# Spreading the first projections of q and k over the score tiles, and turning the last attention sums on TensorE

## The chip, the cores and the metric

The kernel runs on one core of one Trainium2 chip. The metric is the device time of one execution in microseconds. The engines are called as in the profile: PE (TensorE matmuls), PEld (TensorE weight loads), DVE (VectorE), ACT (ScalarE), POOL (GpSimd) and SP (the sync engine, which issues every DMA of this kernel).

## The reference

Two independent attention blocks, A and B, over 2048 tokens of 640 features, with 32 heads of 20 features; their outputs stand side by side.

```
# A: causal attention in a sliding window of 256 tokens
q, k, v = split(x @ wqkv)                      # (heads, S, 20) each
p = softmax(where(0 <= i - j < 256, q k^T * 20**-0.5, -1e9))
a = concat_heads(p @ v) @ wo
# B: linear attention, not causal
phi = lambda t: where(t > 0, t + 1, exp(t)) + 1e-6
kv, z = phi(k)^T @ v, sum(phi(k))
b = concat_heads(phi(q) @ kv / (phi(q) @ z + 1e-6)) @ wo
out = concatenate([a, b], axis=-1)             # (1, 2048, 1280)
```

Inputs, weights and outputs are bf16.

## The kernel before

The tokens are cut into four blocks of 512, numbered 0 to 3 (the first to the fourth block). Everything that can be is a "chain": five matmuls (one for each 128 of the 640 features) that sum into one of four PSUM buffers called `dense`, and then a copy out by VectorE or ScalarE (`evac`, L258 and L260, which share this work by a running allowance). The four buffers go round in turn, so a chain starts only when the chain four places before it has been copied out; the sums of A's attention (`values`) take their place in this ring too.

A's work: `a_rows` makes the rows of q or k of a block in five chains of 512 columns (`qpad`, `kpad`). A head group of four heads needs its rows at 32 row steps, so the first five of eight groups are ready as they come, and the last three are put together by writing spare rows to DRAM and reading them back (`moves`: four writes at L381, four reads at L390). `a_v` makes the values. `scores` makes one of 76 score tiles: matmuls into the one PSUM tile `S_ps` (L747), the exponential by ScalarE (`p`, L765), and the mask by GpSimd's selects (`p` and `plow`, L778). `values` (L805) sums the tiles of a head group over the keys; VectorE turns the result in 32 by 32 squares (`T`, L816), takes the reciprocal (`recA`), and multiplies (`N` and `Nr`, L832). For a block's first 128 features (`N`) four DMA transposes turn the sums to `oT` (`turn_all`, L844); the last 32 of each quadrant (`Nr`) are turned by VectorE (L851). `a_out` multiplies with wo.

B's work: `b_keys` makes phi of the keys, with ScalarE's exponential (`e`, L285) and two steps on VectorE (L290 and L293); `b_sums` sums keys and tokens, `b_kv` and `b_merge` fold the result into the weights (`wB`); `b_q` makes phi of the queries, turned to tokens by DMA (`tok`, L684); `b_den` makes the denominators (`rden`); `quotients` multiplies them in on VectorE (L719), turns each part back by DMA (`xA`, L723); `b_out` makes the output rows.

The order is written out by hand. Ahead of the loop the kernel loads, regroups the weights of q and k into 32 row steps (`regroup`, L356 to L362), and makes all ten chains of the first block of q and k (`run(a_rows(n, 0))`), and drops its eight reads (`drop`). Then the loop over the 76 tiles issues a tile's scores, the sums of the group that was completed two tiles before, and then "fill": chains and other steps taken from a list `plan`, sorted by a due time in tiles (`at`, `do`, `reads_of`, `divide`), until a credit of columns is used up:

```
rate = (FILL - TAIL + n_values * VALUES) / len(units)
```

So FILL is the number of columns in the plan, and TAIL what is kept for the end. After the last tile `take(7000)` runs more fill while the last exponential and masks are made; then come the last sums, the rest of the fill, and `a_out_last`, the output rows of A's fourth block, in chains of 320 columns. Steps that must not run at once (the second half of phi, a reciprocal, a DMA that waits for a copy) are held for one to three chains (`later`, `soon`, `settle`, `flush`).

Of the kernel before, what the change touches and what calls it, by code (L numbers as in the profile page):

```python
# [20 lines left out]
SB = 512  # L21
TPS = SB // P

FILL = 377960
TAIL = 24000

VALUES = 2200
SPARE = 1200
# [62 lines left out]
def kernel(  # L91
# [135 lines left out]
    def flush(before=None):  # L227

        while later and (before is None or later[0][0] <= before):
            later.pop(0)[1]()  # L230
# [33 lines left out]
    def bank(wide=False):  # L264
        flush(begun[0] - 2)
        begun[0] += 1
        settle(False)
        if wide:
            return dps.tile([P, 2 * SB], BF16, name="dense")
        return dps.tile([P, SB], F32, name="dense")  # L270
# [33 lines left out]
    def banks(g, n):  # L304

        for _ in range(n):
            for c in g:
                yield c
                if isinstance(c, End):
                    break  # L310
# [64 lines left out]
    def moves(n, s, pad):  # L375
# [17 lines left out]
            )  # L393

        reads[n, s] = [(read, j) for j in range(4)]

    def drop(key):
        while reads[key]:
            fn, j = reads[key].pop(0)
            fn(j)  # L400

    def a_rows(n, s):
        i = 0 if n == "q" else 1
        pads, pl, name = (q_pad, qp, "qpad") if n == "q" else (k_pad, kp, "kpad")
        pad = pads[s] = pl.tile([P, NG, SB], BF16, name=name)
        for c in range(KT):
            ps = bank()
            yield from chain(
                ps[:],
                lambda kt: wqk[:, i, kt, c * P : (c + 1) * P],  # L410
                lambda kt: xA[s][:, kt, :],
                SB,
            )
            evac(pad[:, c, :], ps[:])
            if c == KT - 1:
                moves(n, s, pad)
            yield End(SB)
# [74 lines left out]
    def wo_proj(wt, base, oT, s, col0):  # L492
        osb = op.tile([P, TPS, D], BF16, name="osb")

        def done(tb, ps):
            if tb is None:
                evac(osb[:, :, SB:D], ps)
            else:
                evac(osb[:, tb, 0:SB], ps[:])

        yield from tok_rows(oT, wt, base, done)
        dst = out2[s * SB : (s + 1) * SB, col0 : col0 + D]
        soon(
            lambda: nc.sync.dma_start(out=dst.rearrange("(t p) n -> p t n", p=P), in_=osb[:]), 2
        )
# [283 lines left out]
    def values(s, g, held):  # L789


        O_ps = dps.tile([P, SB], F32, name="dense")
        todo = []
        for (_, rel, q0, n, col, step), (p, low) in held:
            if rel == "M":
                own = key(s, q0 // P)
                todo.append((own, low, q0, n, col - LOW, step))
                if own >= 2:
                    todo.append((own - 2, p, q0 + HALF, n, col, step))
            else:  # L800
                todo.append((key(s, rel), p, q0, n, col, step))
        for i, (kb, p, q0, n, col, step) in enumerate(todo):
            at = (kb % TPS * H + 4 * g) * HV
            for j in range(4):
                nc.tensor.matmul(  # L805
                    O_ps[32 * j : 32 * (j + 1), q0 : q0 + n],
                    lhsT=v_flat[kb // TPS % 3][:, at + j * HV : at + j * HV + 32],
                    rhs=columns(p, j, col, n, step),
                    start=(i == 0),
                    stop=(i == len(todo) - 1),  # L810
                    tile_position=(0, 32 * j),
                    skip_group_check=True,
                )

        T = tp.tile([P, SB // 32, 32], F32, name="T")
        nc.vector.transpose(out=T.rearrange("p b e -> p (b e)"), in_=O_ps[:])  # L816
        if s not in norm_A:
            norm_A[s] = (
                np_.tile([P, SB // 32, P], BF16, name="N"),
                np_.tile([P, SB // 32, 32], BF16, name="Nr"),  # L820
            )
        N, Nr = norm_A[s]

        def rest():
            r = sp.tile([P, SB // 32, 1], F32, name="recA")
            nc.vector.reciprocal(out=r[:], in_=T[:, :, DH:HV])
            lo = g * DH
            for dst, a, b in ((N, lo, min(lo + DH, P)), (Nr, max(lo, P), lo + DH)):
                if a >= b:
                    continue  # L830
                at = a - P if dst is Nr else a
                nc.vector.tensor_tensor(  # L832
                    out=dst[:, :, at : at + b - a],
                    in0=T[:, :, a - lo : b - lo],
                    in1=r[:].to_broadcast([P, SB // 32, b - a]),
                    op=ALU.mult,
                )
            if lo < P <= lo + DH:
                oT_A[s] = op1.tile([P, KT, SB], BF16, name="oT")

                def turn_all():
                    for j in range(4):
                        quadrant = slice(32 * j, 32 * (j + 1))
                        nc.sync.dma_start_transpose(  # L844
                            out=oT_A[s][:, j, :].rearrange("p (b e) -> p b e", e=32),
                            in_=N[quadrant].rearrange("p b x -> p (b x)"),
                        )

                soon(turn_all, 2)
            if g == NG - 1:  # L850
                nc.vector.transpose(  # L851
                    out=oT_A[s][:, KT - 1, :], in_=Nr.rearrange("p b e -> p (b e)")
                )

        later.append((begun[0], rest))

    def a_out(s):
        settle()
        yield from wo_proj(wo_sb["A"], 0, oT_A[s], s, 0)

    def a_out_last(s):
        settle()
# [16 lines left out]
    def run(gen):  # L879
        for _ in gen:  # L880
            pass
# [39 lines left out]
    def late_load(n, w):  # L921
# [18 lines left out]
        else:  # L940
# [2 lines left out]
            nc.sync.dma_start(out=wo_sb[n][0:g, 0:KT, :], in_=whole)  # L943
            nc.sync.dma_start(out=wo_sb[n][0 : D - KT * g, KT, :], in_=w[KT * g : D, :])

    for n in "qk":
        run(a_rows(n, 0))
    for n in "qk":
        drop((n, 0))


    plan = []
# [1 line left out]
    def at(t0, t1, gen, n):  # L954
        for i in range(n):
            plan.append((t0 + (i + 0.5) / n * (t1 - t0), gen, i == n - 1))
# [9 lines left out]
    def reads_of(t0, t1, n, s):  # L966
        def one():
            fn, j = reads[n, s].pop(0)
            fn(j)

        do(t0, t1, [one] * 4)
# [1 line left out]
    def divide(t0, t1, s):  # L973
        do(t0, t1, [lambda fn=fn, tb=tb: fn(tb) for fn, tb in quotients(s)])

    for s, tq, tk, tv in ((1, (0, 6), (5, 11), (9, 14.5)), (2, (19, 26), (25, 32), (15, 22)),
                          (3, (36, 41.5), (41, 46), (43, 49))):
        at(*tq, a_rows("q", s), KT)
        reads_of(tq[1] + 1.5, tq[1] + 3.5, "q", s)
        at(*tk, a_rows("k", s), KT)  # L980
        reads_of(tk[1] + 1.5, tk[1] + 3.5, "k", s)
        at(*tv, a_v(s), 2 * TPS)
    for s, t0, t1 in ((0, 2, 9), (1, 8.5, 14), (2, 21.8, 27), (3, 27, 32.5)):
        at(t0, t1, b_keys(s), KT)
    for half, t0, t1 in ((0, 15, 21.5), (1, 33.6, 39.2)):
        at(t0, t1, b_sums(half), KT + 2)
    for s, t in ((0, 4), (1, 9), (2, 23), (3, 24)):
        do(t, t, [lambda s=s: load_tok(s)])
    at(40.4, 42, b_kv(), 2)
    do(42.8, 44.8, [lambda c=c: kv_ready(c) for c in range(3)])  # L990
    for s, tq, td, tx in ((0, (39.5, 45), 47, (49, 51)), (1, (45, 50), 53.4, (55.5, 58)),
                          (2, (51.5, 56.5), 59.6, (62, 64.5)), (3, (58.7, 62.8), 65, (66.5, 68.5))):
        at(*tq, b_q(s), KT)
        at(td, td + 0.1, b_den(s), 1)
        divide(*tx, s)
    at(46.5, 54, b_merge(), 2 * KT)
    for n, s, t0, t1 in (("A", 0, 44.5, 48.5), ("A", 1, 51.5, 55.5), ("B", 0, 55.5, 59.5),
                         ("B", 1, 60.5, 64.5), ("B", 2, 65, 68.8), ("A", 2, 68.8, 72.5),
                         ("B", 3, 72.5, 76)):
        at(t0, t1, (a_out if n == "A" else b_out)(s), KT)  # L1000
    for n, s, t0, t1 in (("B", 1, 3, 8), ("A", 2, 6, 12), ("B", 2, 14, 18), ("A", 3, 16, 24),
                         ("B", 3, 17, 22)):
        parts(t0, t1, n, s)
    for s, t0, t1 in ((0, 2, 33.5), (1, 10, 38.5), (2, 20, 45.5), (3, 26, 51.2)):
        do(t0, t0, [lambda s=s: keep_x(s)])
        do(t1, t1, [lambda s=s: again_x(s)])
    for t, n, w in ((13, "B", 2), (20, "B", 0), (40.6, "A", A_wo), (42, "B", B_wo)):
# [13 lines left out]
    def take(cols):  # L1021
        done = 0.0
        while done < cols:
            try:
                done += next(fill)
            except StopIteration:
                break
        return done
# [26 lines left out]
        credit -= take(credit)  # L1055
    spare[0] = None
    while ready:
        take(7000)
        _, at = ready.popleft()
        values(*at, held.pop(at))  # L1060
        flush()
    for _ in fill:
        pass
    flush()
# [30 lines left out]
```

## Time and profile before

| | |
|---|---|
| three runs | 271.9, 274.4 and 275.42 us, median 274.4 |
| the profiled execution | 271.8 us, of which the span from first to last instruction is 270.1 |
| granted TensorE clock, mean | 0.994 |
| busy: PE, PEld | 254.1 and 142.2 us |
| busy: DVE, ACT, POOL | 164.1, 212.2 and 172.8 us |
| first score matmul | 23.62 us |
| first matmul of the last tile's scores | 248.28 us |
| first chain of A's last output rows | 261.1 us |

Times of the profile count from the first instruction. A busy engine may still be one that works below its best, since ends of matmuls are modelled. A releaser in brackets behind a row is what ended the idle time just before that row. The loop runs from 23.62 us to about 250, 3.0 us for a tile; the front holds the loads and the first chains, and the tail the last output rows.

### The profile page before, as it was taken

To read this page: it belongs to the slowest core of one execution; us is meant where nothing else is said; L and a number is where in the kernel's file an instruction comes from. 1 tells how busy PE (TensorE), PEld (TensorE's weight loads), DVE (VectorE), ACT (ScalarE), POOL (GpSimd) and SP (SyncE) were. 2 spreads that over 40 slices of the span, in tenths; PEclk is the share of its full clock that TensorE was granted. 3 is DMA by queue.
4 is the path that set the end of the run, shared out by engine and by line. 5 is a ranking of instruction groups with operands and counts; after the bars stand their busy time and mean duration, and the time that the engine had idled before them with its cause. 6 is when DMAs were issued, how large, how long until landed. Compare 5 with 4: busy or idle time off the path is not lost.

```text
span 270.1 us, 10767 instructions
## 1 busy us (share of the span) xinstructions
PE 254.1 (94%) x4753; PEld 142.2 (53%) x4753; DVE 164.1 (61%) x268; ACT 212.2 (79%) x290; POOL 172.8 (64%) x211
## 2 busy tenths in 40 slices
PE   8899999899999999999999999999599989967995
PEld 7544445465548455454576455565245564534663
DVE  1532476946312458887544663548948979998742
ACT  2455999998999899987778999999468989876221
POOL 6211768878695867676685889595934977776100
PEclk9999999999999999999999999999979999999999
DMA  7994986797369936021652694307573495467574
GB/s 205 302 264 72 198 209 153 195 203 88 61 101 258 237 140 162 12 47 32 96 173 56 125 123 136 60 22 168 105 173 63 132 137 107 83 120 167 141 156 177
DMA packets 67683, 36.87 MB, mean 137 GB/s; under 512 B 50357, under 2 KB 66613, under 8 KB 67637
## 3 DMA queue, kind: packets, MB, share of 16 engines
q1 hardware_dynamic: 67637, 36.19, 60.6%
q8 instruction: 37, 0.61, 1.0%
q14 instruction: 9, 0.07, 0.1%
HBM read 14.42 MB, written 9.83 MB: 90 GB/s over the span
## 4 chain that ended last, share of the span: by engine, by line
PE 72%; DVE 14%; DMA 4%; POOL 3%; ACT 3%; issue 3%; SPq 1%; DVEq 0%; ACTq 0%
PE dense L275 46%; PE dense L547 9%; PE S_ps L747 9%; PE dense L805 7%; DVE tok L719 3%; DVE e L290 3%; DVE phi L293 3%; DMA wA<-in_A_wqkv_dram 2%; ACT p L765 2%; POOL p L778 2%; DMA xA<-tok 2%; DVE N L832 1%; POOL plow L778 1%; DVE T L816 1%; PE dense L626 1%
## 5 line engine op out<-in xcount | busy, mean ns | idle before, releaser
L778 POOL TENSOR_SCALAR_AFFINE_SELECT p<-p 128x512 bf16<-128x512 bf16 (+1 forms) x152 | 123.1, 819 | 69.6 <-ACT p L765 64.4
L765 ACT ACTIVATE p<-S_ps 128x2048 bf16<-128x2048 f32 x76 | 142.2, 1872 | 22.2 <-PE S_ps L747 21.7
L275 PE MATMUL dense<-xA,wqk 128*128 128x512 bf16 x200 | 49.5, 380 | 0.0
L290 DVE TENSOR_SCALAR e<-e 128x512 bf16<-128x512 bf16 x40 | 28.2, 704 | 29.5 <-ACT e L285 26.2
L778 POOL TENSOR_SCALAR_AFFINE_SELECT plow<-p 128x1024 bf16<-128x1024 bf16 x32 | 39.9, 1248 | 2.2
L275 PEld LDWEIGHTS <-xA 128*128 128x128 bf16 x320 | 26.8, 98 | 23.3 <-DMA xA<-tok 4.7
L816 DVE STREAM_TRANSPOSE T<-dense 128x512 f32<-128x512 f32 x32 | 22.6, 708 | 24.4 <-PE dense L805 24.4
L747 PE MATMUL S_ps<-qpad,kpad 20*64 20x64 bf16 (+3 forms) x1728 | 35.4, 214 | 0.1
L747 PEld LDWEIGHTS <-kpad 20*64 20x64 bf16 (+1 forms) x1728 | 17.6, 100 | 30.2 <-issue 25.8
L275 PEld LDWEIGHTS <-wqk 128*128 128x128 bf16 x200 | 18.4, 98 | 20.6 <-issue 1.1
L275 PE MATMUL dense<-wo,oT 128*128 128x512 bf16 (+2 forms) x160 | 26.5, 307 | 2.9 <-DVE wB L260 2.8
L805 PE MATMUL dense<-p,vA 128*32 128x64 bf16 (+2 forms) x1152 | 27.4, 223 | 1.7 <-POOL p L778 0.9
L293 DVE SCALAR_TENSOR_TENSOR phi<-dense,e 128x512 bf16<-128x512 f32 x40 | 27.7, 692 | 1.7
L258 ACT ACTIVATE osb<-dense 128x512 bf16<-128x512 f32 (+1 forms) x26 | 14.6, 571 | 16.6 <-PE dense L275 14.5
L275 PE MATMUL dense<-wA,xA 128*128 128x320 bf16 x160 | 26.6, 300 | 1.0 <-DVE phi L293 0.4
L275 PE MATMUL dense<-wB,xA 128*128 128x512 bf16 (+1 forms) x160 | 23.9, 299 | 3.8 <-DMA xA<-tok 3.8
L275 PE MATMUL dense<-wB,xB 128*128 128x512 bf16 (+1 forms) x160 | 26.9, 300 | 0.1
L547 PE MATMUL dense<-phi,tok 128*128 128x512 bf16 (+1 forms) x160 | 25.6, 300 | 0.5 <-DVE phi L293 0.5
L275 PE MATMUL dense<-xB,wB 128*128 128x512 bf16 x100 | 25.9, 380 | 0.0
L805 PEld LDWEIGHTS <-vA 128*32 128x32 bf16 x1664 | 22.3, 96 | 4.7 <-issue 1.6
L285 ACT ACTIVATE e<-dense 128x512 bf16<-128x512 f32 x40 | 23.7, 593 | 0.1
L832 DVE TENSOR_TENSOR N<-T,recA 128x320 bf16<-128x320 f32 (+1 forms) x28 | 20.2, 721 | 1.0
(62 smaller groups left out, 224.0 us busy)
## 6 DMA issues: line engine op xcount, KB each, us to landing
out_dram<-osb SPq DMA_DIRECT2D x7, 640.0 KB
x_scr<-xB SPq DMA_DIRECT2D x4, 640.0 KB
tok<-in_B_x_dram SPq DMA_DIRECT2D x4, 640.0 KB
xB<-x_scr SPq DMA_DIRECT2D x4, 640.0 KB
wB<-in_B_wqkv_dram SPq DMA_DIRECT2D x3, 800.0 KB
q_scr<-qpad SPq DMA_DIRECT2D x16, 60.0 KB
k_scr<-kpad SPq DMA_DIRECT2D x16, 60.0 KB
qpad<-q_scr SPq DMA_DIRECT2D x16, 60.0 KB
```

The source lines that it names most:

```text
L258: nc.scalar.activation(out=dst, in_=src, func=ACT.Copy)
L275: nc.tensor.matmul(dst, lhsT=lhs(kt), rhs=rhs(kt), start=(kt == 0), stop=(kt == KT - 1))
L285: nc.scalar.activation(out=view(e), in_=src, func=ACT.Exp)
L290: nc.vector.tensor_scalar(out=e[:], in0=e[:], scalar1=1e-6, scalar2=1.0 + 1e-6, op0=ALU.add, op1=ALU.min)
L293: nc.vector.scalar_tensor_tensor(out=dst, in0=src, scalar=0.0, in1=view(e), op0=ALU.max, op1=ALU.add)
L547: nc.tensor.matmul(out, lhsT=lhs(x, pk)[:, tb, :], rhs=rhs(pk, tb), start=(i == 0), stop=(i == len(blocks) - 1),)
L747: nc.tensor.matmul(columns(S_ps[k0:k1], j, col, n, step), lhsT=kt[32 * j : 32 * j + DH, g, ko + k0 : ko + k1], rhs=q_pad[s][32 * j : 32 * ...
L765: nc.scalar.activation(out=p, in_=S_ps[:], func=ACT.Exp, scale=scale)
L778: nc.gpsimd.affine_select(out=dst, in_=src, pattern=[[0, 4], [0, n // HALF], [sgn, HALF]], compare_op=ALU.is_ge, fill=0.0, base=base, chan ...
L805: nc.tensor.matmul(O_ps[32 * j : 32 * (j + 1), q0 : q0 + n], lhsT=v_flat[kb // TPS % 3][:, at + j * HV : at + j * HV + 32], rhs=columns(p, ...
L816: nc.vector.transpose(out=T.rearrange("p b e -> p (b e)"), in_=O_ps[:])
L832: nc.vector.tensor_tensor(out=dst[:, :, at : at + b - a], in0=T[:, :, a - lo : b - lo], in1=r[:].to_broadcast([P, SB // 32, b - a]), op=AL ...
```

## The change

Of the ten chains of the first block of q and k only two, one of each, are made ahead of the loop. The other eight go into the plan at due times -0.5 to 3.6, and the eight reads, which `drop` issued before, follow at 5 to 6. FILL grows by 20480, which is 8 chains of 5 matmuls of 512 columns. For A's fourth block the four DMA transposes are left out; `turn_last` turns N with 16 matmuls against the identity into two `dense` buffers, copied to `oT` by VectorE and ScalarE, right after the last sums. TAIL falls by 11000 columns, `take(7000)` becomes `take(5500)`, and the outputs change places: B's fourth block comes before A's third, which is now the one in the tail. Due times of steps between move by up to two tiles.

```
-FILL = 377960
-TAIL = 24000
+FILL = 398440
+TAIL = 13000
...
-    def drop(key):
-        while reads[key]:
-            fn, j = reads[key].pop(0)
-            fn(j)
...
                 def turn_all():
+                    if s == NS - 1:
+                        return
...
+    def turn_last(s):
+
+        for b0 in (0, 8):
+            ps = bank(wide=True)
+            for b in range(8):
+                nc.tensor.transpose(
+                    ps[:, b * P : (b + 1) * P], norm_A[s][0][:, b0 + b, :], ident[:]
+                )
+            dst = oT_A[s][:, 0:4, b0 * 32 : (b0 + 8) * 32].rearrange("p j (b q) -> p j b q", q=32)
+            src = ps[:].rearrange("p (b j q) -> p j b q", j=4, q=32)
+            if b0:
+                nc.scalar.activation(out=dst, in_=src, func=ACT.Copy)
+            else:
+                nc.vector.tensor_copy(out=dst, in_=src)
...
+    first_rows = {n: a_rows(n, 0) for n in "qk"}
     for n in "qk":
-        run(a_rows(n, 0))
-    for n in "qk":
-        drop((n, 0))
+        run(banks(first_rows[n], 1))
...
-    for s, tq, tk, tv in ((1, (0, 6), (5, 11), (9, 14.5)), (2, (19, 26), (25, 32), (15, 22)),
+    for n, t in (("q", 0), ("k", 0.1)):
+        at(t - 0.5, t + 3.5, first_rows[n], KT - 1)
+        reads_of(t + 5, t + 6, n, 0)
+    for s, tq, tk, tv in ((1, (2.2, 8), (7, 12), (10, 15)), (2, (19, 26), (25, 32), (16, 22)),
                           (3, (36, 41.5), (41, 46), (43, 49))):
...
-    for s, t0, t1 in ((0, 2, 9), (1, 8.5, 14), (2, 21.8, 27), (3, 27, 32.5)):
+    for s, t0, t1 in ((0, 4, 10), (1, 10, 15), (2, 21.8, 27), (3, 27, 32.5)):
         at(t0, t1, b_keys(s), KT)
-    for half, t0, t1 in ((0, 15, 21.5), (1, 33.6, 39.2)):
+    for half, t0, t1 in ((0, 16.4, 21.5), (1, 33.6, 39.2)):
         at(t0, t1, b_sums(half), KT + 2)
-    for s, t in ((0, 4), (1, 9), (2, 23), (3, 24)):
+    for s, t in ((0, 6), (1, 11), (2, 23), (3, 24)):
         do(t, t, [lambda s=s: load_tok(s)])
...
-                          (2, (51.5, 56.5), 59.6, (62, 64.5)), (3, (58.7, 62.8), 65, (66.5, 68.5))):
+                          (2, (51.5, 56.5), 59.6, (61, 63.5)), (3, (58.2, 62.2), 64, (65.5, 67.5))):
         at(*tq, b_q(s), KT)
         at(td, td + 0.1, b_den(s), 1)
         divide(*tx, s)
...
-                         ("B", 1, 60.5, 64.5), ("B", 2, 65, 68.8), ("A", 2, 68.8, 72.5),
-                         ("B", 3, 72.5, 76)):
+                         ("B", 1, 60.2, 64), ("B", 2, 64.4, 68.2), ("B", 3, 69, 73),
+                         ("A", 2, 73, 76)):
         at(t0, t1, (a_out if n == "A" else b_out)(s), KT)
-    for n, s, t0, t1 in (("B", 1, 3, 8), ("A", 2, 6, 12), ("B", 2, 14, 18), ("A", 3, 16, 24),
+    for n, s, t0, t1 in (("B", 1, 5, 9), ("A", 2, 6, 12), ("B", 2, 14, 18), ("A", 3, 16, 24),
                          ("B", 3, 17, 22)):
         parts(t0, t1, n, s)
-    for s, t0, t1 in ((0, 2, 33.5), (1, 10, 38.5), (2, 20, 45.5), (3, 26, 51.2)):
+    for s, t0, t1 in ((0, 2, 33.5), (1, 12, 38.5), (2, 20, 45.5), (3, 26, 51.2)):
...
-        take(7000)
+        take(5500)
         _, at = ready.popleft()
         values(*at, held.pop(at))
         flush()
+    turn_last(NS - 1)
     for _ in fill:
         pass
```

## The prediction

> **What bounds the kernel now.** I read four views in this order: the page for who is busy, a table of windows for where TensorE stands still, the chain that ended last for why, and the timeline for the places the edit touches. "Tile k" is the k-th of the 76 score tiles, counted from 0; its stretch runs from its first score matmul (S_ps L747) to the next tile's. In the timeline, tile 0 starts at 23.62, tile 55 at 180.67, tile 60 at 200.68, tile 73 at 238.54, tile 75 at 248.28.
>
> ```profile
> span 270.1 us, 10767 instructions
> PE 254.1 (94%) x4753; PEld 142.2 (53%) x4753; DVE 164.1 (61%) x268; ACT 212.2 (79%) x290; POOL 172.8 (64%) x211
> ```
>
> TensorE is busy 94% of the span, so only 16.0 us of it can be waiting. The windows say where (columns: us, busy us of PE, PEld, DVE, ACT, POOL with counts, granted clock, DMA share, GB/s).
>
> ```profile
> 0.00:12.73 12.73, 10.38 (x91) 8.27 (x92) 3.91 (x8) 4.73 (x9) 5.65 (x19) 1.00 0.91 255
> 12.73:23.62 10.89, 10.89 (x52) 4.80 (x50) 4.32 (x9) 4.58 (x7) 1.14 (x4) 1.00 0.95 208
> 23.62:180.67 157.05, 155.18 (x3160) 85.65 (x3160) 86.44 (x150) 142.30 (x192) 116.06 (x136) 1.00 0.58 125
> 180.67:200.68 20.01, 16.36 (x305) 8.42 (x305) 15.29 (x24) 14.50 (x23) 13.37 (x15) 0.91 0.59 124
> 200.68:238.54 37.86, 36.98 (x825) 20.64 (x824) 34.27 (x50) 33.88 (x44) 26.38 (x30) 1.00 0.54 111
> 238.54:248.28 9.74, 5.91 (x86) 2.94 (x87) 9.24 (x11) 6.22 (x9) 8.84 (x8) 1.00 0.81 164
> 248.28:270.10 21.82, 18.41 (x248) 11.44 (x247) 10.58 (x19) 6.02 (x9) 1.35 (x3) 1.00 0.59 156
> ```
>
> Tiles 0 to 54 waste only 157.05 - 155.18 = 1.9 us. Tiles 55 to 59 waste 3.65 us and run at a mean clock of 0.91, which is another 20.01 x 0.09 = 1.8. Tiles 60 to 72 waste 0.9, tiles 73 and 74 waste 3.8. Together 10.3 us in tiles 55 to 74, where VectorE is the busy one (34.27 of 37.86). The first chains (12.73 to 23.62) waste nothing. The chain and the timeline give the two causes of the late waits.
>
> ```profile
> 189.44 2.65 DVE tok L719 x2
> 192.08 0.40 DVE wB L260
> 192.49 1.28 DVE tok L719
> ...
> 195.37 0.39 DVE wB L260
> 195.80 1.44 PE dense L275 x3
> ```
>
> ```profile
> 240.27 1.25 PE L275 MATMUL dense<-wB,xA 128*128 128x512 bf16 x5 [1.18 <-DMA xA<-tok]
> 242.64 1.25 PE L275 MATMUL dense<-wB,xA 128*128 128x512 bf16 x5 [1.12 <-DMA xA<-tok]
> 245.76 2.37 PE L275 MATMUL dense<-wB,xA 128*128 128x512 bf16 x25 [1.53 <-DMA xA<-tok]
> ```
>
> First: the chains share four PSUM buffers "dense", so a chain waits until the buffer of the fourth one before it is emptied. VectorE empties wB (L260) only after the multiplies of L719 ahead of it in its queue, and TensorE stands 2.83 us before 195.80. Second: the output of B's third block waits for its transposed rows, which follow the same multiplies.
>
> **The change, part by part.** The sum is made against the profiled execution, 271.8 us by the clock outside, which is its span of 270.1 and 1.7 around it. That execution lies 1% under the median of 274.4.
>
> *Eight chains move.* Fifty matmuls take 10.96 us, 0.219 each. Forty of them leave the front and return between tiles 0 and 4: 8.8 us out, 8.8 us in, zero in itself, since TensorE is busy on both sides. Lists of instructions in program order show them there. What changes is what the two chains left in front wait for.
>
> ```profile
> 12.73 10.96 PE L275 MATMUL dense<-xA,wqk 128*128 128x512 bf16 x50
> 13.27 1.86 ACT L356 ACTIVATE wqk<-kpad 128x2000 bf16<-128x2000 bf16 x1
> 23.73 0.60 ACT L258 ACTIVATE kpad<-dense 128x512 bf16<-128x512 f32 x1 [1.56 <-PE dense L275]
> ```
>
> Four chains of q used to cover the regrouping of k's weights. Now k's first chain is second: q ends at 12.73 + 1.10 = 13.83, the weights are ready at 13.27 + 1.86 = 15.13, a wait of 1.3. k ends at 16.2, and tile 0 now needs that very result, copied in 0.60, so it starts at about 17.0 instead of 23.62 - 8.8 = 14.85. Cost +2.1 (1.4 if the copy is hidden, 2.4 with wider gaps). The row before 195.80 shows a half clock after 2.83 us of standing; if these two waits did that too, 1.7 more would come. I leave it out, as each is under half of 2.83.
>
> The Trainium skill, "TensorE: Matmul & The Clock Gate", section "What's actually happening", states half rate only after an idle window of about 3.4 us. By it the front costs nothing more, by the row's worst reading the sum would be 1.7 higher.
>
> *Writes and reads of the first rows.* They leave a gap of nothing and join the sync queue behind tiles 4 to 6: 4 + 4 writes, 8 reads, one transposed load of B's second block between them. Rows of before: four writes 1.58 to 2.10, four reads 1.48 to 2.01, a transposed load 2.65. Issued from about 17.0 + 6 x 3.0 = 35, that is 35 + 2.1 + 2.0 + 1.5 + 2.7 = 43, and some 1.5 for landing; tile 10 needs them at 17.0 + 10 x 2.95 = 46.5. Cost 0, with 2 us of cover. Behind them the parts of B's second block come later (to about 46), used at tile 11 (49). The other loads shift by up to two plan units; none of theirs ends a wait of TensorE in before.
>
> *Early waits.* Of 1.9 us in tiles 0 to 54 some 0.5 should go, since B's phi work is spread over more tiles. -0.5 (-1.9 to +2).
>
> *Turning A's last sums.* Four DMA transposes (5.79 us of SP from 252.24) go, which lay behind the 6.2 us of chains from 254.93 to 261.1 and gain nothing. Sixteen transposes come: ten of the same kind (L177) took 0.73 us, so 0.9 to 1.2, I take 1.0, on TensorE's path. Two copies of 1024 columns follow: 640 took 0.49 on VectorE and 0.70 on ScalarE, so 0.7 to 1.2. They lie beside the chains of A's third block that are left (7100 columns, 3.0 us), after the last transposition of Nr (0.72 + 0.25 + 0.49 + 0.71 after the last sums); without that cover 1.0 more.
>
> *Tail.* TAIL falls from 24000 to 13000 and the rate per tile rises from 5584 to 5998 columns. By counting columns, tile 75 and what follows needs 3.5 us less of TensorE and tiles 55 to 74 3.5 more: zero in itself. The last output buffer then waits for the DMA of B's fourth block instead of A's third, issued about 4 us into tile 75 and wanted at 10; before, ScalarE waited 2.06 us at 262.83 for such a DMA. Cost 0 (to +1).
>
> *The late stretch*, where the sum is decided. Counting VectorE's list from the copy of wB ahead of the first multiply to the sixteenth multiply: 77 instructions before, 78 after, the same kinds. In before this strand takes 185.27 to 247.77 = 62.5 us (55.4 busy up to 247.5). What moves is where it stands: the sixteenth multiply sits in tile 74 before and in tile 72 after. Before, tiles 55 to 74 last 67.6 us, 57.3 of work and 10.3 of waits; after they hold 60.8 of work.
>
> From below: the strand starts 3.1 us into tile 55, lasts 62.5, its rows land about 3.1 later (1.2 to issue, 1.5 to 2.4 to land, from the rows around 240), and 1.4 of chains follow: 70.1 us. From above I go through the buffers. At tile 56 the list puts wB, recA, N, Nr, e, phi (0.48 + 0.25 + 0.34 + 0.35 + 0.66 + 0.69 and gaps of 0.2) ahead of the buffer that the next chain needs: ready at 6.05 where TensorE arrives at 3.5, a wait of 2.5. Then three multiplies, wB, a fourth, e and phi stand ahead of A's second output: with 1.36 each (the rows at 189 to 193) a wait of 5.2, with the fastest (0.78) 3.2, I take 4.0, and 1.7 for the clock. That is 8.2 at this place against 5.4. Going on so, with mean durations, gives 75.1 for the stretch. B's third block has its multiplies about three tiles ahead of its chains instead of two and should lose most of its 3.8 us; B's fourth, which moves from the tail into tiles 73 to 75, picks some of it up. Between 70.1 and 75.1 I take 72.3: TensorE waits 11.5 instead of 10.3. Cost +1.2 (-1.0 to +4.0).
>
> **Sum.** 2.1 - 0.5 + 1.0 + 1.2 = +3.8: a span of 273.9, an execution of 275.6. That is 1.4% above its own base and inside the 2% that a measurement of this kernel can tell from no change. Runs in the upper part of before's spread would give 278.
>
> **Rivals.** (1) *VectorE's strand sheds idle time; not slower.* The strand holds 62.2 - 55.4 = 6.8 us without work, waits for TensorE among them, and its e (L290) takes 0.28 to 1.24, its multiply 0.78 to 1.76, long ones while POOL selects. More chain work per tile feeds it sooner. If it sheds half, 3.5, tiles 55 to 74 take 66.6, the late term is -4.5 and the time 269.9. It decides from a strand under 60.9 us, where the sum is zero. For it: POOL has 2.2 us a tile either way, over longer tiles. Against it: four multiplies now sit together, where before had one, two and one.
>
> The Trainium skill, "SBUF — State Buffer", section "Who interferes with whom", has VectorE with two SBUF inputs and a GpSimd read exclude each other for a whole instruction. By it, a multiply that meets a 0.67 us select takes up to 0.78 + 0.67 = 1.45, an estimate; that speaks against this rival.
>
> (2) *B's fourth block pays, and the clock drops twice; slower.* Its chains at tile 73 stand one to two tiles behind their multiplies, as the third block's did. The stretch reaches the walk's 75.1 and another half-clock spell adds 1.7: 76.8, late term +5.7, time 280.1. For it: transposed rows landed 2.4 to 3.1 us apart at 240 to 246. Against it: nothing else of VectorE is left in tiles 73 and 74 (two copies and an N).
>
> (3) *First rows late.* If eight reads wait for landings one by one, tile 10 stands 3 us: 278.6. Against it: in before all writes and reads were through in 24.35 to 29.51.
>
> **How the numbers follow.** Sum 0.48 (own range 272 to 279; 0.35 within 2%, 0.13 slower), rival 1 0.25 (0.17 within, 0.08 faster), rival 2 0.19 (0.17 slower, 0.02 within), rival 3 0.08 (0.06 slower, 0.02 within). Faster 0.08, within 0.56, slower 0.36. The range runs from below rival 1 to above rival 2, with the spread of before's runs: 267.5 to 283.
>
> **What would show it.** Right: tile 0 at 17.0 with a 1.3 us gap ahead of k's first chain; no wait at tile 10; a wait of 2 to 3 and one of about 4 us at tiles 56 and 57 with a half-clock spell; no DMA wait of B's third block above 1 us; sixteen transposes in about 1 us. Wrong: tiles 55 to 74 under 68.5 us (rival 1) or over 75 (rival 2), or tile 0 later than 18.

## The result: 0.5% faster, and most of that is the clock

The kernel after takes 270.62 us (median of 22 runs, 269.07 to 273.21), the kernel before 273.44 beside it (22 runs, 269.98 to 278.44). The ratio is 0.9946, with a 95% interval of 0.992 to 0.9972; executions more than 1.5% above their kernel's fastest beside them are left out of it, as of the table below, which is why it lies nearer to one than the ratio of the two medians (0.990). Faster by half a per cent: I had forecast 1.4% slower than the profiled execution.

The head of the page and the windows of the profiled execution after, cut at the same tiles as before (tile 0, 55, 60, 73 and 75):

```profile
span 268.0 us, 10800 instructions
PE 254.9 (95%) x4769; PEld 143.1 (53%) x4769; DVE 157.1 (59%) x267; ACT 214.8 (80%) x293; POOL 171.0 (64%) x211
```

```profile
0.00:12.70 12.70, 11.24 (x93) 9.02 (x94) 4.15 (x9) 4.94 (x10) 5.69 (x20) 1.00 0.89 263
12.70:16.77 4.07, 2.09 (x9) 0.62 (x8) 1.31 (x4) 2.65 (x4) 1.09 (x4) 1.00 1.09 271
16.77:181.32 164.55, 163.99 (x3210) 89.68 (x3210) 87.72 (x154) 146.55 (x200) 116.97 (x137) 1.00 0.58 126
181.32:201.16 19.84, 17.00 (x302) 8.78 (x302) 13.94 (x26) 14.29 (x20) 11.33 (x14) 0.91 0.65 140
201.16:243.92 42.76, 39.66 (x841) 21.86 (x841) 38.68 (x57) 35.04 (x46) 27.58 (x30) 1.00 0.65 127
243.92:249.99 6.07, 6.07 (x84) 3.06 (x83) 1.63 (x4) 5.45 (x9) 5.80 (x7) 1.00 0.77 162
249.99:268.00 18.01, 14.87 (x240) 10.10 (x238) 9.63 (x18) 5.84 (x8) 2.58 (x4) 1.00 0.31 111
```

Line by line against before: tile 0 starts at 16.77 instead of 23.62. Tiles 0 to 54 take 164.55 instead of 157.05, and TensorE waits 0.6 us there instead of 1.9. Tiles 55 to 59 take 19.84 (before 20.01), again at a mean clock of 0.91. Tiles 73 and 74 wait for nothing (6.07 busy of 6.07; before 5.91 of 9.74). The end takes 18.01 instead of 21.82. In sum -6.85 + 7.50 - 0.17 + 1.24 - 3.82 = -2.1 us of span (the fourth term is tiles 60 to 74, 48.83 instead of 47.60).

VectorE's work fell too, from 164.1 to 157.1 us, with one instruction fewer: between the copy of wB ahead of its first multiply and its sixteenth multiply, the twelve e (L290) take 7.03 us together instead of 9.57, and the sixteen multiplies 17.94 instead of 19.69.

Each run also gives its span and mean granted clock. Span times (1 - clock) estimates the time lost to the lower clock, as if TensorE were at work through all of it, and span times clock is the rest. The runs of before beside the result have no clock on record, so its row takes the 51 runs beside the experiments; means in us:

| kernel | runs | span | lost to the clock | rest |
|---|---|---|---|---|
| before | 51 | 270.92 | 2.75 | 268.16 |
| after | 21 | 268.48 | 1.01 | 267.47 |
| spread only | 11 | 271.65 | 3.78 | 267.87 |
| late part only | 11 | 270.33 | 2.83 | 267.50 |
| DMA turn | 12 | 271.11 | 1.75 | 269.36 |
| three chains in front | 6 | 264.18 | 0.09 | 264.10 |
| rate only | 11 | 269.77 | 2.53 | 267.25 |
| multiplies apart | 6 | 263.25 | 1.10 | 262.15 |
| before, TensorE kept at work | 12 | 268.86 | 0.11 | 268.75 |
| buffers in turn | 6 | 283.17 | 4.86 | 278.30 |

The standard error of "rest" is 0.2 in the first two rows and 0.3 to 0.5 in the others, and before's own three sets of runs average 267.75, 268.14 and 268.50, so a difference under 0.7 us should not be built on. Of the 2.4 us between before and after, 1.7 are clock (standard error 0.3) and 0.7 are left for the schedule. None of the 21 runs after has a clock under 0.99; 21 of the 51 before have. Outside the span after takes 2.1 us and before 1.7, so the 2.4 us of span are 2.1 of time; the result's own runs of before give 1.5.

The profiled execution of after is one of its better ones: its span times clock is 266.3, 1.1 us under its mean, while that of before, 268.4, is 0.2 over its mean. One half-clock spell is in each of the two, so of the -2.1 us above some 1.3 are the luck of these two executions.

### The profile page after: what moved, and what is told of

Same layout as the page of the kernel before. It is cut to its first block, busy times and chain, and to the rows that moved or that the text cites. A ratio compares the mean times of both kernels' runs of the same rounds, so it can differ in the third digit from the quotient of the medians.

```text
span 268.0 us, 10800 instructions
## 1 busy us (share of the span) xinstructions
PE 254.9 (95%) x4769; PEld 143.1 (53%) x4769; DVE 157.1 (59%) x267; ACT 214.8 (80%) x293; POOL 171.0 (64%) x211
## 4 chain that ended last, share of the span: by engine, by line
PE 77%; DVE 7%; DMA 5%; ACT 4%; POOL 3%; issue 2%; SPq 1%; DVEq 0%
PE dense L275 49%; PE dense L542 9%; PE S_ps L742 9%; PE dense L800 8%; DVE tok L714 3%; DMA wA<-in_A_wqkv_dram 2%; POOL p L773 2%; ACT p L760 2%; DVE e L290 2%; DMA xA<-tok 2%; DMA out_dram<-osb 1%; DVE N L827 1%; POOL plow L773 1%; DVE phi L293 1%; ACT wqk L356 1%
## 5 line engine op out<-in xcount | busy, mean ns | idle before, releaser
L275 PE MATMUL dense<-xA,wqk 128*128 128x512 bf16 x200 | 50.1, 380 | 1.3 <-ACT wqk L356 1.3
L290 DVE TENSOR_SCALAR e<-e 128x512 bf16<-128x512 bf16 x40 | 25.0, 625 | 32.4 <-ACT e L285 22.0
L773 POOL TENSOR_SCALAR_AFFINE_SELECT plow<-p 128x1024 bf16<-128x1024 bf16 x32 | 38.8, 1211 | 2.2
L275 PE MATMUL dense<-wB,xA 128*128 128x512 bf16 (+1 forms) x160 | 25.3, 300 | 0.5 <-DMA xA<-tok 0.4
L275 PE MATMUL dense<-wo,oT 128*128 128x512 bf16 (+2 forms) x160 | 25.2, 304 | 0.4 <-ACT p L736 0.4
L542 PE MATMUL dense<-phi,tok 128*128 128x512 bf16 (+1 forms) x160 | 24.9, 300 | 0.0
L827 DVE TENSOR_TENSOR N<-T,recA 128x320 bf16<-128x320 f32 (+1 forms) x28 | 19.0, 678 | 1.0
```

The source lines that it names most:

```text
L275: nc.tensor.matmul(dst, lhsT=lhs(kt), rhs=rhs(kt), start=(kt == 0), stop=(kt == KT - 1))
L290: nc.vector.tensor_scalar(out=e[:], in0=e[:], scalar1=1e-6, scalar2=1.0 + 1e-6, op0=ALU.add, op1=ALU.min)
L542: nc.tensor.matmul(out, lhsT=lhs(x, pk)[:, tb, :], rhs=rhs(pk, tb), start=(i == 0), stop=(i == len(blocks) - 1),)
L773: nc.gpsimd.affine_select(out=dst, in_=src, pattern=[[0, 4], [0, n // HALF], [sgn, HALF]], compare_op=ALU.is_ge, fill=0.0, base=base, chan ...
L827: nc.vector.tensor_tensor(out=dst[:, :, at : at + b - a], in0=T[:, :, a - lo : b - lo], in1=r[:].to_broadcast([P, SB // 32, b - a]), op=AL ...
```

## The experiments

The first four asked where the gain comes from. I worked out the table above only after them; their expectations speak of spans and medians.

**Spread only** (after, its late part undone, so that the four DMA transposes of A's fourth block are back as well):

```
-TAIL = 13000
+TAIL = 24000
...
-(2, (51.5, 56.5), 59.6, (61, 63.5)), (3, (58.2, 62.2), 64, (65.5, 67.5))
+(2, (51.5, 56.5), 59.6, (62, 64.5)), (3, (58.7, 62.8), 65, (66.5, 68.5))
...
-("B", 1, 60.2, 64), ("B", 2, 64.4, 68.2), ("B", 3, 69, 73), ("A", 2, 73, 76)
+("B", 1, 60.5, 64.5), ("B", 2, 65, 68.8), ("A", 2, 68.8, 72.5), ("B", 3, 72.5, 76)
...
-        take(5500)
+        take(7000)
...
-                    if s == NS - 1:
-                        return
...
-    turn_last(NS - 1)
```

> The changed kernel with its late part undone: the eight chains are spread and the early due times moved, but TAIL is 24000 again, the last sums of A are turned by DMA, and the outputs stand in their old order and times. Theory L (the gain comes from the late part: multiplies and outputs that stand better, so that waits for transposed rows go): this kernel keeps the front's cost (+2.0 us) and the early waits that went (-1.3), so 0 to +1.0 us on before, ratio 1.000 to 1.004, and tiles 73 and 74 still wait 3 to 4 us for transposed rows. Theory E (the gain comes from the spread itself, which gives ScalarE and VectorE work earlier): -1.5 to -2.5 us, ratio 0.991 to 0.995.

Measured: 273.84 us, ratio 1.0031 (0.9994 to 1.0068). Tile 0 starts at 17.1, but tiles 73 and 74 wait again for B's rows. The span went up to 272.9, with a second spell of half clock:

```profile
179.27:200.92 21.65, 16.43 (x297) 8.69 (x297) 15.84 (x23) 14.43 (x23) 12.85 (x15) 0.92 0.57 109
239.22:250.68 11.46, 9.04 (x89) 3.71 (x89) 6.36 (x9) 5.50 (x8) 8.52 (x8) 0.70 0.60 130
```

These are tiles 55 to 59 and 73 to 74, with clocks of 0.92 and 0.70: 89 matmuls are busy 9.04 us where after has 6.07 for 84. So the chains' move alone does not bring the gain.

**Late part only** (before, with the lines above turned the other way and `turn_last` put in):

> The kernel before with the late part alone: TAIL 13000, the sums of A's fourth block turned by TensorE, the outputs in the new order and the late due times; all ten first chains stay in front. Theory L: the late gain without the front's cost, -2 to -3.5 us, ratio 0.987 to 0.993, no wait over 1 us for transposed rows in tiles 73 and 74. Theory E: the sixteen transposes cost 1.0 us and nothing comes back, 0 to +1 us, ratio 1.000 to 1.004.

Measured: 272.45 us, ratio 0.9989 (0.9948 to 1.003): no difference that can be told, between the two expectations. Tiles 73 and 74 no longer wait, but a stand of 3.16 us came up at tile 69, where the timeline of TensorE has

```profile
235.10 0.56 PE L696 MATMUL dense<-zk,phi 128*128 128x8 bf16 x16 [3.16 <-DVE phi L293]
```

and a half-clock spell followed at 237.0. Taken as ratios, neither part brings anything and both together do: 1.0031 x 0.9989 = 1.002 against 0.9946. The table resolves it. In "rest" the parts are worth -0.29 and -0.66, together -0.95 against -0.69 measured, well within their errors. What does not add up is the lost clock: 3.78 and 2.83 in the parts, 2.75 in neither, 1.01 in both.

**DMA turn** (after, A's last sums turned by the four DMA transposes):

```
-                    if s == NS - 1:
-                        return
...
-    turn_last(NS - 1)
```

> The changed kernel, only that the sums of A's fourth block are turned by four DMA transposes again. Theory of a needed step (with only 5300 columns of chains left, the DMA's 5.8 us of issue are no longer covered): the last output rows of A wait 1.5 to 2.5 us, minus 0.9 for the transposes saved, +0.6 to +1.6 us on the changed kernel. Rival (the DMA is hidden here as well): 0.9 us faster than the changed kernel, whose ratio to before is 0.9946.

Measured: 273.08 us, ratio 0.9985 (0.9947 to 1.0024). Against after that is 1.1 us by the two ratios and 2.6 us by the spans of the table: the step was needed, and its size stays open. The end, tile 75 onward, takes 19.45 instead of 18.01: three chains wait for the transposes,

```profile
258.75 0.31 PE L275 MATMUL dense<-wo,oT 128*128 128x320 bf16 x1 [0.81 <-DMA oT<-N]
259.23 0.31 PE L275 MATMUL dense<-wo,oT 128*128 128x320 bf16 x1 [0.17 <-DMA oT<-N]
260.17 2.08 PE L275 MATMUL dense<-wo,oT 128*128 128x320 bf16 x14 [0.63 <-DMA oT<-N]
```

In before no chain waited for these transposes (TensorE is busy without a gap from 254.9 to 262.8), since chains lay beside them; with TAIL at 13000 that cover is gone, and the sixteen matmuls at 1.0 us are the cheaper way. The turn by TensorE belongs to the shorter tail; that it would gain nothing without one follows from the rows of before, and was not run.

**Three chains in front** (three in all, one more than after: a second chain of q is made ahead of the loop, which covers the regrouping of k's weights; q's other chains fall due one tile later, and FILL is smaller to match):

```
-FILL = 398440
+FILL = 395880
...
-    for n in "qk":
-        run(banks(first_rows[n], 1))
+    run(banks(first_rows["q"], 2))
+    run(banks(first_rows["k"], 1))
...
-        at(t - 0.5, t + 3.5, first_rows[n], KT - 1)
+        if n == "q":
+            at(0.5, 3.5, first_rows[n], KT - 2)
+        else:
+            at(t - 0.5, t + 3.5, first_rows[n], KT - 1)
```

> The changed kernel with two chains of q and one of k ahead of the loop (FILL smaller by 2560 columns), so that q's second chain covers the regrouping of k's weights. Theory of an additive front: the wait of 1.30 us ahead of k's first chain falls to about 0.2, and the execution by 1.0 us on the changed kernel, ratio to before about 0.991. Rival (later waits take up what the front gives): the front starts as told, and the time stays at 0.9946.

Measured: 266.04 us, ratio 0.9702 (0.9651 to 0.9753), far more than the 1 us I expected. The front is as worked out: tile 0 at 16.45 with one chain more ahead of it, the wait for the weights down from 1.30 to 0.22 us.

```profile
14.43 1.24 PE L275 MATMUL dense<-xA,wqk 128*128 128x512 bf16 x5 [0.22 <-ACT wqk L356]
16.45 0.40 PE L742 MATMUL S_ps<-qpad,kpad 20*128 20x256 bf16 x8 [0.79 <-DVE kpad L260]
```

Of the 4.3 us of span between the two rows of the table, the front is 1.4 (0.32 earlier, with a chain of 1.1 more) and the clock 0.9 (the six runs lose 0.09 us in the mean). The other 2.0 stay open. The two traces can't place them: they differ by 3.4 us, of which front and clock are 2.8, and the profiled execution of after is 1.1 us better than its mean.

**Rate only** asks whether that shift of the late steps, without the covered front, brings the gain:

```
-FILL = 398440
+FILL = 395880
```

> The kernel after with one number changed: FILL is 395,880 instead of what it was, so that the interleaved steps are dealt out at 5,964 columns of a tile instead of 5,998; no chain is moved, so tile 0 starts where it does after (16.8 us) and TensorE has the same work. Theory A (the version with three more front chains was faster by 4.6 us on the median for its covered front, some 1 us, and for a loop that by luck had no half-clock spell): this version stays where the kernel after is, 0.990 to 0.998 of before. Theory P (the multiplies' and the late chains' places against each other decide: a small shift of the late steps removes waits): the waits of tiles 55 to 74 in the profile go from 8 us to about 4, as in that version, and the ratio to before is 0.975 to 0.987.

Measured: 271.66 us, ratio 0.998 (0.9939 to 1.002); "rest" is 267.25, as after. Theory P falls: the rate alone brings nothing, and its profile has a spell at 235.97. Theory A has the time about right (the upper edge of its band), but does not explain the whole 4.6 us: what goes beyond front and clock stays open.

**Multiplies apart** (three chains in front, and the due times of VectorE's multiplies moved):

```
...
-(0, (39.5, 45), 47, (49, 51)), (1, (45, 50), 53.4, (55.5, 58)), (2, (51.5, 56.5), 59.6, (61, 63.5))
+(0, (39.5, 45), 46.4, (46.9, 51.5)), (1, (45, 50), 53, (53.6, 58.2)), (2, (51.5, 56.5), 59.2, (59.8, 63.8))
...
```

> The version with the three front chains (0.970 of before), with VectorE's multiplies by the denominators set further apart: the steps of tile block 0 due from 46.4, of block 1 from 53, of block 2 from 59.2, so that no three of them run in a row. In that version the profile still has 3.1 us of waits in tiles 55 to 59 and 3.2 in 60 to 72, all behind a multiply on VectorE. Theory V (the late waits are the length of a run of multiplies): these waits fall to 2 to 4 us together and the ratio to before is 0.958 to 0.968. Rival (each multiply holds up the next chain by its own length, in a row or not): the waits stay at 6 us or grow, and the ratio is 0.968 to 0.978.

Measured: 265.02 us, ratio 0.9719 (0.9662 to 0.9775), the same as with three chains in front; the rival's numbers. The multiplies of the first block no longer run together, and tiles 55 to 59 fall from 17.97 to 16.88 us, but tiles 60 to 72 grow from 41.78 to 43.82, with a new stand and a half-clock spell behind it (mean clock 0.96):

```profile
203.97 0.59 PE L275 MATMUL dense<-wB,xA 128*128 128x512 bf16 x2 [1.69 <-DVE osb L260]
```

These two versions are the fastest here, and their ratios can't be told from each other. In "rest" the second is 2.0 us lower, of which the two sets of before beside them differ by 0.75, so a gain of the schedule that the clock took back is not ruled out.

**No multiplies**, before and after (the sixteen multiplies by the denominators left out):

```
-            nc.vector.tensor_tensor(
-                out=vh, in0=vh, in1=rden_of[s][:, tb, :, :].to_broadcast([P, H, DH]), op=ALU.mult
-            )
+            if tb == 0:
+                nc.vector.tensor_copy(out=ones[:], in_=rden_of[s][:, 0, 0, :])
```

> The kernel before without the 16 multiplies of the output rows by the reciprocal denominators on VectorE; their results are left out of the output, all the rest runs. Theory V (the late waits come from these multiplies): TensorE's waits in tiles 55 to 74, some 11 us in the profile of before, fall under 3 us, no half-clock spell appears, and the span is 258 to 263 us. Rival (they come from the chains' own buffers and the late transfers): the waits of tiles 73 and 74 (4 us) and at least half of the others stay, span over 265.

> The kernel after without the same 16 multiplies (their results are left out of the output, all the rest runs). Theory V: the waits of tiles 55 to 74, 8 us in the profile of after, fall under 2 us, no half-clock spell, span 258 to 262 us: so the two kernels without multiplies differ by under 2 us, the change's own share in front and tail. Rival (the chains now moved into the tiles cause waits of their own there): 4 us or more stay, span over 264.

Only the product is left out; one small copy for each block of tokens keeps the reciprocals read. Measured in one run each: spans of 263.6 and 266.5. Tiles 55 to 59, first of before and then of after, without the multiplies:

```profile
181.07:196.57 15.50, 14.55 (x302) 8.13 (x304) 10.51 (x21) 14.07 (x22) 11.00 (x14) 1.00 0.56 121
```

```profile
181.24:197.93 16.69, 15.27 (x298) 8.04 (x301) 10.43 (x23) 14.15 (x20) 10.84 (x14) 1.00 0.59 125
197.93:241.78 43.85, 39.86 (x833) 21.93 (x841) 27.20 (x49) 35.00 (x46) 23.69 (x30) 0.96 0.73 139
```

The stands of tiles 55 to 59, with their half clock, went with the multiplies (20.01 to 15.50, 19.84 to 16.69). Those behind did not. Before keeps 2.5 us of waits in tiles 73 and 74 of 3.8, and 4.2 in tiles 55 to 74, so it meets theory V in the missing spell and misses its 3 us. After keeps a wait of 2.26 us at tile 70, for a DMA, and a spell after it (clock 0.96): over 4 us of waits stay and the span is over 264, which is the rival's forecast.

```profile
232.40 1.04 PE L275 MATMUL dense<-wB,xA 128*128 128x512 bf16 x3 [2.26 <-DMA xA<-tok]
```

The chain at 232.40 is the first of B's third block, whose waits lay in tiles 73 and 74 before: its transposed rows are wanted earlier now, and without the multiplies they still come late there. In the kernel after itself the waits at tile 70 are for VectorE's phi and osb (1.0 and 0.6 us).

**TensorE kept at work** tests the clock by itself, on the kernel before: matmuls whose result the next chain overwrites, at the places where TensorE stands (`again` is 4 for B's third block, else 0).

```
+                for _ in range(14 if c == 3 and lo else 0):
+                    nc.tensor.matmul(ps[:, 0 : D // 2], ..., start=True, stop=True)
...
+            for _ in range(again if tb else 0):
+                nc.tensor.matmul(ps[:], lhsT=xt[:, 0, (tb - 1) * P : tb * P], ...)
```

> The kernel before with 26 matmuls added that compute nothing new (each is overwritten by the chain that follows it), put where TensorE stands in its profile: 14 of 320 columns (0.134 us each, 1.9 us) in the chain ahead of the 2.83 us wait at tile 58, and four of 512 columns (0.9 us) ahead of each of the three chains of tiles 73 and 74 that wait 1.1 to 1.5 us for transposed rows. No wait ends earlier; only the standing is shorter. Of the runs so far, spans times granted clock average 268.2 us before and 267.3 after, and the time lost to a lower clock 3.05 against 1.27 us. Theory C (most of the gain of the kernel after is half-clock time that it avoids, and the stands at these two places bring it about): the mean loss here falls under 1.5 us, span times clock stays at 267.5 to 269, and the ratio to before is 0.992 to 0.997. Rival (the lower clock comes whether or not TensorE stands there, or the added matmuls delay the chains): loss over 2.5 us, or span times clock over 269, ratio 0.999 to 1.006.

Measured: 270.44 us, ratio 0.9914 (0.9883 to 0.9945), from adding 26 useless matmuls. The lost clock falls from 2.75 to 0.11 us, "rest" rises from 268.16 to 268.75, and the span is 2.1 us shorter. Theory C holds, and its size was set a little too low. At the first place TensorE's timeline reads

```profile
192.67 2.06 PE L657 MATMUL dense<-wo,kv_T 120*128 120x320 bf16 x14 [0.26 <-DVE wB L260]
...
195.93 0.81 PE L275 MATMUL dense<-wo,oT 128*128 128x512 bf16 x2 [0.93 <-DVE wB L260]
```

The useless matmuls (L657) take 1.9 of the 2.83 us; the chain behind starts at 195.93 instead of 195.80, so nothing was waited for any less, and the matmuls behind it run at full clock. In tiles 73 and 74 only one of three waits is left, 0.25 us.

**Buffers in turn** tests the step of the prediction that failed most (next section): after, with four pools of one buffer each, taken round (in the built program all 220 buffers after the first four are the one of four places before).

```
-    dps = pool("dps", 4, PSUM)
+    four = [pool(f"dps{i}", 1, PSUM) for i in range(4)]
...
+            self.n += 1
+            return four[(self.n - 1) % 4].tile(*a, **k)
```

> The kernel after, its four dense PSUM buffers given out strictly in turn (a pool of one buffer for each, taken round), as the prediction's walk through the buffers took it; nothing else changed. Theory W (the walk was right for buffers in turn, and failed because the kernel after does not give them out so): in the profile TensorE waits 2 to 3 us at tile 56 and 3 to 5 at tile 57 instead of 0.6 and 1.6, tiles 55 to 59 take 22 to 25 us instead of 19.8, and the ratio to before is 1.000 to 1.012. Rival (the walk's durations were too long, whatever the order of the buffers): tiles 55 to 59 stay at 19 to 21 us, and the ratio at 0.992 to 0.998.

Measured: 284.96 us, ratio 1.0446 (1.0406 to 1.0487). Tiles 55 to 59 take 24.99 us, and two chains, both in tile 56 here, wait where the prediction's walk had it, 1.94 and 3.12 us for its 2.5 and 4.0:

```profile
196.97 1.24 PE L284 MATMUL dense<-xB,wB 128*128 128x512 bf16 x5 [1.94 <-DVE phi L302]
198.04 0.98 PE L658 MATMUL dense<-wo,kv_T 120*128 120x320 bf16 x6
202.15 1.01 PE L284 MATMUL dense<-wo,oT 128*128 128x512 bf16 x2 [3.12 <-DVE phi L302]
```

```profile
196.83 3.20 DVE L723 TENSOR_TENSOR tok<-tok,rden 128x640 bf16<-128x640 bf16 x3
199.96 0.48 DVE L269 CAST wB<-dense 128x320 bf16<-128x320 f32 x1
200.36 0.81 DVE L723 TENSOR_TENSOR tok<-tok,rden 128x640 bf16<-128x640 bf16 x1
201.09 0.28 DVE L299 TENSOR_SCALAR e<-e 128x512 bf16<-128x512 bf16 x1
201.40 0.69 DVE L302 SCALAR_TENSOR_TENSOR phi<-dense,e 128x512 bf16<-128x512 f32 x1
```

That is the list of the prediction, step for step: three multiplies, wB, a fourth, e and phi, ahead of A's second output. Theory W holds for this place. The whole ratio is far above its band, because with the same order tiles 0 to 54 take 174.2 us instead of 164.6, of which I had thought nothing.

## Why the prediction was wrong, by its own steps

Predicted and measured, in us of span against before (the 8.8 us of chains and the 3.5 us of columns that change places taken out, as in the prediction):

| step | predicted | measured | how |
|---|---|---|---|
| front waits | +2.1 | +1.95 | 16.77 - (23.62 - 8.8) |
| early waits | -0.5 | -1.3 | 164.55 - 157.05 - 8.8 |
| late stretch | +1.2 | -2.4 | 68.67 - 67.60 - 3.5 |
| turn and end | +1.0 | -0.3 | 18.01 - 21.82 + 3.5 |
| sum | +3.8 | -2.1 | |

These are single executions. In the means of the table the sum is -2.4: the forecast missed by 6.2 us, 1.7 in the clock, which had no term, and 4.5 in the schedule. The measured time lies between rival 1's 269.9 and the sum's 275.6, inside the range, but the direction was forecast wrongly.

**Front: right.** The two waits stand where they were put (1.30 and 0.69 us), no clock was lost by them in this run, and no row of q or k was late at tile 10. Some of the agreement is luck: from the first chain of q (at 12.30 here, at 12.73 in before) to tile 0 the change costs 4.47 - (10.89 - 8.8) = 2.4 us, and the chain's earlier start hides 0.4 of it.

```profile
14.84 1.24 PE L275 MATMUL dense<-xA,wqk 128*128 128x512 bf16 x5 [1.30 <-ACT wqk L356]
16.12 0.60 ACT L258 ACTIVATE kpad<-dense 128x512 bf16<-128x512 f32 x1 [1.42 <-PE dense L275]
16.77 0.40 PE L742 MATMUL S_ps<-qpad,kpad 20*128 20x256 bf16 x8 [0.69 <-ACT kpad L258]
```

The version with three chains shows that this wait was not necessary.

**Early waits and end: sizes.** The early waits went, 0.8 us more of them than forecast; the end came out 1.3 us better, and with the other sign. The transposes themselves took the 1.0 us of the sum, as the chain of the end shows:

```profile
256.23 1.00 PE dense L863 x16
```

TensorE's other work there fell by 4.5 us (18.41 busy before, 14.87 less these 1.0 after), not by the 3.5 that I counted, and 0.3 us less of it is idle.

**Late stretch: the step that failed.** "From above I go through the buffers" took the four PSUM buffers to go round in turn, as the section on the kernel before says too. They don't: in both kernels a chain gets the buffer that was chosen for it when the program was built, and this order is not a round one. Of the 220 buffers after the first four, only 126 are the one of four places before in the program of after, and 128 of 218 in that of before. TensorE after, at the place of the predicted waits of 2.5 and 4.0 us:

```profile
184.72 1.25 PE L275 MATMUL dense<-xB,wB 128*128 128x512 bf16 x5
185.81 0.71 PE L649 MATMUL dense<-wo,kv_T 120*128 120x320 bf16 x4
186.73 0.43 PE L649 MATMUL dense<-wo,kv_T 120*128 120x320 bf16 x2 [0.20 <-DVE phi L293]
187.59 0.59 PE L275 MATMUL dense<-wo,oT 128*128 128x512 bf16 x2 [0.43 <-ACT p L736]
...
190.24 0.25 PE L800 MATMUL dense<-plow,vA 128*32 128x64 bf16 x4 [1.58 <-DVE wB L260]
```

The chain at 184.72 starts at once, although VectorE's recA, N, Nr, e and phi run from 184.9 to 186.7, in the order predicted: its buffer was last that of sums whose matmuls ended at 182.54, three places before it. A's second output (187.59) got the buffer of a wB whose matmuls ended at 186.25, and does not wait for the multiplies at all; only the sums of tile 57 do, for a wB behind three multiplies:

```profile
186.59 3.20 DVE tok L714 x3
189.79 0.41 DVE wB L260
```

The waits of tiles 55 to 59 were 2.84 us in after, where the prediction had 6.5 and the kernel with buffers in turn has 7.28. So the queue on VectorE was read rightly (its steps ran a little shorter than reckoned) and the coupling to TensorE was assumed. With the 1.7 us of the half clock, which did come, that is 4.5 instead of 8.2: the whole miss of 3.6 us in the late stretch of this execution. Tiles 60 to 74 waited 3.1, as much as the 11.5 - 8.2 = 3.3 that the sum left for them.

**B's third and fourth block.** The third block, now at 236.27 to 243.1, lost its waits but for one of 0.37 us, as predicted. That the fourth "picks some of it up" was wrong: VectorE's last multiply ends at 243.79, ahead of tile 73, and the chains of that block wait for nothing.

**The rivals.** Rival 1 (VectorE's strand sheds time) came nearest: the strand went from 62.5 to 59.3 us, under its deciding 60.9, and tiles 55 to 74 took 68.67 (its edge was 68.5). Its reason was half wrong: the strand holds more idle time than before (8.2 against 6.8 us), not less, and is shorter because the same e and multiplies took 4.3 us less. GpSimd's selects beside them took somewhat less too: 873 against 889 ns in the mean for `p`, two fewer, and 1288 against 1415 ns for the eight of `plow`. The Trainium skill, "SBUF — State Buffer", section "Who interferes with whom", has VectorE and GpSimd shut each other out at a shared port; a multiply of 0.78 to 1.77 us fits with that, though the longest is above the prediction's estimate of 1.45, and no run here took the selects away, so why VectorE's steps were shorter stays open. Rivals 2 and 3 did not happen: no wait of B's fourth block that counts, none at tile 10.

**The clock.** The prediction priced one half-clock spell on each side and let it cancel, because the profile of before has just one. It took one profiled execution for the kernel: this one lost 1.7 us where the kernel before loses 2.75 in the mean. The change's effect on how often the clock falls was the largest term of its result (-1.7 of -2.4), and had no term in the sum. The stands were in the tables I read: three of 1.12 to 1.53 us within 6 us at tiles 73 and 74 were counted as waits only.

## What to carry to other kernels

Stands of TensorE have two prices, the wait and, by chance, a spell of half clock after it; the second is seen only over many runs, so read the granted clock of every run and not that of the one profile, and note that a few useless matmuls in place of a stand can pay. Before walking a queue through shared buffers, take from the built program which buffer each step really gets. A wait that a first chain leaves in front is worth covering: the version with one chain more there gained more than the whole change, though only 2.3 of its 4.3 us are accounted for.

## What was not expected of the hardware

A half-clock spell lasts 3.41 us or twice that (6.83 in "spread only"), and the stretches between spells are whole multiples of 3.41 us as well (71.68 = 21 x 3.41 in before). Laid on that grid in the twelve traces, each of the ten spells inside the kernels follows a stretch of 3.41 us in which TensorE stood between 1.5 and 2.8 us, and no stretch with more than 1.94 us of standing was without one; between 1.5 and 1.94 both happened. Two like traces differ by where the grid falls: after stood 1.56 us from 188.68 and got a spell, "DMA turn" the same 1.56 us from 188.74 and got none. The Trainium skill, "TensorE: Matmul & The Clock Gate", section "What's actually happening", says that the window runs freely, with 3413 ns, which these traces agree with, and that the half rate comes after an idle window; here about half a window of standing was enough, and the measurement decides. The prediction cited that rule as one reason to price the front's waits at nothing more: after's 1.30 and 0.69 us did go without, but "buffers in turn" had a spell at 17.5 us behind the same two waits. There both fell into one stretch of 3.41 us, 1.99 us in all; in after the grid parted them. So that the front lost no clock in after was luck too.
